# Attention with a mixture of depths on one core: another order of the last products, rows updated product by product, and one scatter a batch

## The chip, the cores and the metric

The kernel runs on one core of a Trainium2 chip. The metric is device microseconds (us) of one execution, less is better. The kernel before was timed three times: 689.43, 689.62 and 692.24 us, with a median of 689.62 us. One more execution was recorded by the hardware profiler. It took 691.44 us in all, of which the trace covers a span of 689.6 us. Moments "at 650.35" are us from the start of that span.

## The reference

```python
# attention with pooled queries: B=8 batches, H=8 heads, S=1152 keys, D=64
q_pool = q.reshape(B, H, S // 2, 2, D).mean(axis=3)          # 576 queries
scores = scale * np.matmul(q_pool, k.transpose(0, 1, 3, 2))
attn = np.exp(scores - max); attn = attn / (sum + 1e-09)
x = np.matmul(attn, v)                                       # -> (B, 576, 512)
# mixture of depths: per batch the 128 best rows go through two dense layers
scores = np.einsum('bsd,d->bs', x, w_gate)
for b in range(B):
    top_idx = np.argpartition(-scores[b], 128)[:128]
    xe = x[b, top_idx]
    h = np.maximum(xe @ w1, 0.0)                             # 512 -> 1024
    ye = h @ w2                                              # 1024 -> 512
    g = 1.0 / (1.0 + np.exp(-scores[b, top_idx]))
    out[b, top_idx] = xe + g[:, None] * ye
```

Everything is float32.

## The kernel before

The order of the work is written out by hand. Each engine runs its instructions in the order in which the program emits them, and waits on semaphores where data come from another engine.

**Main loop** (`run`). Two heads form a pair, and a pair is worked in two halves of 288 queries. Each half has, on TensorE (PE), the scores (L871, 72 records) and the weighted values of the half before (L889, 72 records). ScalarE (ACT) takes the exponential of the scores (L878) and copies the weighted values out (`two`, L897). GpSimd (POOL) adds score tiles (`acc`, L910), adds the two queries of each pool (`qp`, L769), forms the products for the gate (`prod`, L978) and divides (`x`, L1015, `divided`). VectorE (DVE) folds the sums (`fold`, L915) and transposes keys and queries (`kT`, L772, and `qT`, L776). SyncE (SP) issues the loads of keys, queries and values and the stores of `x`, in one queue. PE's next scores need `kT` and `qT`.

**Routing of a batch** (`routed`, a generator). After a batch's last pair its scores are laid out in one line (`line` on DVE; `groups` by four ACT copies, L940; `total` on DVE), written to DRAM and read back to all partitions. DVE ranks them by counting (L1116, L1125, L1135), the 128 best rows are fetched with an indirect DMA on POOL (L1227) and their transpose `xeT` is made. The generator stops at marks: `"mid"`, `"sums"` and `True` (end of the half) say where in the next half the main loop takes it up again (`units`). So work of the routing is spread over later halves, at places fixed by the marks.

**The dense layers** take two batches at once, with Strassen's scheme in Winograd's form: seven products of half-size quarters in place of eight. The text numbers them as the changed kernel does: P1 = a11·b11, P2 = a12·b21, P3 = s1·t1, P4 = s2·t2, P5 = s3·t3, P6 = s4·b22, P7 = a22·t4. The `s` are four sums of quarters of the input, the `t` are sums of weights made early in the kernel, kept in DRAM and loaded into `tw` (`load_sums`, two transfers a layer). Results are sums of products. Batches 0 to 3 go through `layers_of_two` inside the main loop. There, in the kernel before, ACT scales the four result quarters by the gate (L1419), POOL adds them onto the fetched rows `xe` (L1424), and `written` scatters the rows of each batch to `out` with an indirect DMA (L1303).

**The ending** (`ending`) follows the main loop. It holds four layers: the first and second for batches 4 and 5 ("A" and "B" below), and the first and second for batches 6 and 7 ("C" and "D"); A3 is product P3 of layer A. A product of a first layer is 8 matmuls of 128 columns (L1442, two records each), one of a second layer 4 of 256 columns (L1452). PSUM has room for four products at a time (`banks`). Into these products the ending weaves the ranking and fetch of batch 7 (`new`) and the last steps of batch 6 (`old`). Batch 7's ranking needs two small transfers, DVE's counting, one ACT instruction (`gate`, Exp, L1149), ten matmul records that turn ranks into row numbers (L1186), two ACT copies (L1193, L1194), the indirect fetch (`lines<-out_dram,index`, L1227), and four transposes on PE (L1275). In the kernel before, layer B runs P1, P2, P7, P3, P4, P5, P6, with batch 7's row numbers between P4 and P5; POOL makes B's four sums; all B results are combined during C, scaled on ACT and added on POOL. Layer D runs P1, P2, P7, P3 ... P6, batch 6's rows are scattered in two halves of 256 columns, batch 7's in one piece. A scatter waits until the scatter before it has landed, since both write `out`.

In this ending DVE divides the last two pairs' rows (`divided`, L1015); SP stores them.

Of the kernel before, what the change touches and what calls it, by code (L numbers as in the profile page):

```python
# [10 lines left out]
P = 128  # L11
BLK = 32

G = 3
F32 = mybir.dt.float32
I32 = mybir.dt.int32
AF = mybir.ActivationFunctionType
ALU = mybir.AluOpType
# [516 lines left out]
class _Plain:  # L535
# [473 lines left out]
    def divided(self, pair):  # L1009

        x = pair["x"] = self.work.tile([P, self.QB, BLK], F32, name="x")

        ending = pair["b"] == self.B - 1 and pair["hp"] >= self.NPAIR - 2
        engine = self.nc.vector if ending else self.nc.gpsimd
        engine.tensor_tensor(  # L1015
            out=x[:, :, :],
            in0=pair["avb"][:, :, :],
            in1=pair["rec"][:, :].unsqueeze(2).broadcast_to([P, self.QB, BLK]),
            op=ALU.mult,
        )  # L1020
# [39 lines left out]
    def routed(self, b, part):  # L1060
# [11 lines left out]
        )  # L1072
        sc = ffn.tile([P, NT], F32, name="gate_sc")
        if b < self.B - 1:
            yield mid
        groups = self.side_by_side(line)
        if b < self.B - 1:
            yield True
# [297 lines left out]
    def layers_of_two(self, tokens):  # L1376
# [37 lines left out]
        rest = [room[0:w, i, 0:half] for i in (0, 3, 1)]  # L1414
        c = [of[0:w] for of in (c11, c12, c21, c22)]
        yield from self.seven_products(2, quarters(hidden, self.NFC // 2), s, c, rest, lambda bank: bank[0:w, 0:half])
        yield "mid"
        for i, of in enumerate(c):
            nc.scalar.activation(of, of, AF.Copy, scale=tokens[i // 2]["gate"][0:w, 0:1])  # L1419
        yield True  # L1420
        for i, of in enumerate(c):
            token = tokens[i // 2]
            to = token["xe"][0:w, i % 2 * half : (i % 2 + 1) * half]
            nc.gpsimd.tensor_tensor(out=to, in0=of, in1=to, op=ALU.add)  # L1424
            if i % 2:
                self.written(token, token["index"])
                yield True
        if tokens[1]["b"] + 1 < self.paired:
            for _ in self.load_sums(1):
                yield True  # L1430
# [4 lines left out]
    def product(self, layer, of, by, to):  # L1435
# [16 lines left out]
                self.nc.tensor.matmul(to, lhsT=of[:, k, :], rhs=by[:, k, :], start=k == 0, stop=k == n - 1)  # L1452
        return to

    def add(self, to, x, y):
        self.nc.vector.tensor_tensor(out=to, in0=x, in1=y, op=ALU.add)

    def first_layer(self, a, s, c, m):

        copy = self.nc.scalar.copy
        (a11, a12, _, a22), (s1, s2, s3, s4), (c11, c12, c21, c22), (u, w) = a, s, c, m
        b11, b21, b22 = (self.quarter(1, i, j) for i, j in ((0, 0), (1, 0), (1, 1)))
        t1, t2, t3, t4 = (self.summed(1, i) for i in range(4))

        def product(of, by):
            return self.product(1, of, by, self.banks()[:, 0, :])

        def hidden(to, x, y):  # L1470
            self.add(to, x, y)
            self.nc.scalar.activation(to, to, AF.Relu)

        copy(u, product(a11, b11))
        yield
        hidden(c11, u, product(a12, b21))
        yield
        copy(w, product(s1, t1))
        yield
        self.add(u, u, product(s2, t2))  # L1480
        self.add(w, w, u)
        yield
        ps = product(s3, t3)
        hidden(c22, w, ps)
        self.add(u, u, ps)
        yield
        hidden(c12, w, product(s4, b22))
        yield
        hidden(c21, u, product(a22, t4))
        yield  # L1490

    def second_layer(self, a, s):

        (a11, a12, _, a22), (s1, s2, s3, s4) = a, s
        b11, b21, b22 = (self.quarter(2, i, j) for i, j in ((0, 0), (1, 0), (1, 1)))
        t1, t2, t3, t4 = self.last_sums
        for of, by in ((a11, b11), (a12, b21), (a22, t4), (s1, t1), (s2, t2), (s3, t3), (s4, b22)):
            yield self.product(2, of, by, self.banks()[:, 0, :])

    def row(self, tile):  # L1500
        names = "a b c d"[: 2 * len(tile.shape) - 3]
# [4 lines left out]
        n = tiles[0].shape[1] // 2  # L1506
        return [tile[:, i * n : (i + 1) * n, 0:w] for tile in tiles for i in range(2)]

    def four_sums(self, engine, a, room):

        n, w = a[0].shape[1], a[0].shape[2]
        s = [self.lines_of(room[:, i * n * P : (i + 1) * n * P])[:, :, 0:w] for i in range(4)]
        a11, a12, a21, a22 = a
        s1, s2, s3, s4 = s
        add, subtract = ALU.add, ALU.subtract
        for to, x, y, op in ((s1, a21, a22, add), (s2, s1, a11, subtract), (s3, a11, a21, subtract), (s4, a12, s2, subtract)):
            engine.tensor_tensor(out=to, in0=x, in1=y, op=op)
        return s

    def ending(self, halves, old):  # L1520

# [6 lines left out]
                if i + 1 == n:  # L1528
                    break

        def layer_rooms(room):
            return [self.lines_of(room[:, i * half * 2 : (i + 1) * half * 2])[:, :, 0:w] for i in range(2)]

        tokens, a, s = self.left
        w = tokens[0]["w"]
        self.room = self.row(self.work.tile([P, self.NG, G, 2, self.HALF], F32, name="p"))
        acc = [self.row(self.work.tile([P, G, 2 * self.HALF], F32, name="acc"))]
        tiles = [self.ffn.tile([P, self.NFC, P], F32, name="hT") for _ in tokens]
        c = self.quarters_of(tiles, w)
        layer = self.first_layer(a, s, c, layer_rooms(acc[0]))  # L1540

        self.gated(halves[-3])
        pieces(old, 1)
# [14 lines left out]
        for of in (halves[-3]["pair"], last):  # L1558
            self.divided(of)
            self.stored(of)  # L1560
        pieces(layer, 3)
        pieces(new, 1)
        pieces(layer)
        room = self.ffn.tile([P, 4, 512], F32, name="s", bufs=1).rearrange("p a n -> p (a n)")
        s = self.four_sums(nc.gpsimd, c, room)
        acc.append(self.row(self.work.tile([P, G, 2 * self.HALF], F32, name="acc")))
        at = [acc[1][0:w, i * half : (i + 1) * half] for i in range(6)] + [acc[0][0:w, 4 * half : 5 * half]]
        layer = self.second_layer(c, s)
        for to in at[0:2]:
            copy(to, next(layer))  # L1570
        pieces(new, 2)
        for to in at[2:5]:
            copy(to, next(layer))
        pieces(new, 1)
        pieces(old)
        for to in at[5:7]:
            copy(to, next(layer))
        low = self.counted()

        room = self.row(self.work.tile([P, self.NG, G, 2, self.HALF], F32, name="p"))  # L1580
        n = self.NFC * P
        tiles = [self.lines_of(room[:, i * n : (i + 1) * n]) for i in range(2)]
        room = room[:, 2 * n : 4 * n]
        c = self.quarters_of(tiles, w)
        m = self.room[:, 6 * half : 11 * half]
        xeT = [self.lines_of(self.room[:, i * self.Dm : (i + 1) * self.Dm]) for i in range(2)]
        a = self.quarters_of(xeT, w)
        nxt = [self.lines_of(room[:, i * half : (i + 1) * half])[:, :, 0:w] for i in range(4)]
        layer = self.first_layer(a, nxt, c, layer_rooms(m))
        pieces(layer, 1)  # L1590
        pieces(new)
        self.four_sums(nc.vector, a, room)
        m1, m2, m7, m3, m4, m5, m6 = at
        pieces(layer, 1)
        add(m2, m2, m1)
        add(m4, m4, m1)
        pieces(layer, 1)
        add(m3, m3, m4)
        add(m6, m6, m3)
        add(m3, m3, m5)  # L1600
        pieces(layer, 1)
        add(m4, m4, m5)
        add(m7, m7, m4)
        for i, of in enumerate((m2, m6, m7, m3)):
            nc.scalar.activation(of, of, AF.Copy, scale=tokens[i // 2]["gate"][0:w, 0:1])
            to = tokens[i // 2]["xe"][0:w, i % 2 * half : (i % 2 + 1) * half]
            nc.gpsimd.tensor_tensor(out=to, in0=of, in1=to, op=ALU.add)
            if i % 2:
                self.written(tokens[i // 2], tokens[i // 2]["index"])
        pieces(layer, 2)  # L1610
        count = self.outside(low)
        pieces(layer)
        s = self.four_sums(nc.vector, c, room)

        six, seven = tokens = self.last_tokens
        index = [self.part_of_rows(six, part, 2) for part in range(2)]
        to = [token["xe"][0:w, i * half : (i + 1) * half] for token in tokens for i in range(2)]
        u, v, y, z, own = (m[0:w, i * half : (i + 1) * half] for i in range(5))
        found = nc.values_load(count[0:1, 0:1])
        E = mybir.EngineType  # L1620
        self.tc.mark_branch_hint_location("again", found, [E.PE, E.DVE, E.Pool, E.Activation, E.SP])

        def scaled(to, of, token, plus):
            nc.vector.scalar_tensor_tensor(
                out=to, in0=of, scalar=token["gate"][0:w, 0:1], in1=plus, op0=ALU.mult, op1=ALU.add
            )

        layer = self.second_layer(c, s)
        copy(u, next(layer))
        add(own, u, next(layer))  # L1630
        scaled(to[0], own, six, to[0])
        self.written(six, index[0], 0, 2)
        copy(y, next(layer))
        copy(v, next(layer))
        add(u, u, next(layer))
        add(v, v, u)
        scaled(z, v, six, to[1])
        ps = next(layer)
        add(v, v, ps)
        add(u, u, ps)  # L1640
        scaled(to[3], v, seven, to[3])
        add(y, y, u)
        scaled(to[2], y, seven, to[2])
        self.written(seven, seven["index"])
        scaled(to[1], next(layer), six, z)
        self.written(six, index[1], 1, 2)
        return found

    def counted(self):
# [187 lines left out]
```

## Time and profile before

| | us |
|---|---|
| median of three runs (lowest, highest) | 689.62 (689.43, 692.24) |
| the profiled execution | 691.44 |
| its span | 689.6 |
| PE busy | 673.4 |
| DVE busy | 575.0 |
| POOL busy | 516.7 |
| ACT busy | 458.9 |
| main loop, to the first product of the ending | 0 to 624.9 |
| ending | 624.9 to 689.6 |

Lines of the timeline hold the start in us, the duration, the engine, the line of the program, the operation, what is written and read with its shape, and a count. In square brackets stands how long the engine had been idle before it, and what ended that wait. "PEld" is the weight load of PE, which overlaps its matmuls. "PEclk" is the share of its full clock that PE was granted.

### The profile page before, as it was taken

Reading aid. Unit: us, or ns where it says so; the run is one execution under the profiler, and the core shown is the slowest. Engines: PE = TensorE matmul, PEld = TensorE weight load, DVE = VectorE, ACT = ScalarE, POOL = GpSimd, SP = SyncE. Lnnn points to the kernel's source line nnn. Section 1 sums busy time; section 2 is a strip of 40 time slices with the busy share of each in tenths; the row PEclk is TensorE's granted clock in tenths of the full one; section 3 lists DMA queues with packets and bytes.
Section 4 is the critical chain, followed back from the end, with each engine's and each line's share of the span. In section 5 each row is a group of like instructions: output and inputs, shape, how many; then the busy total and the mean of one; then the engine's idle time right before and its main releaser. Section 6 shows DMA issues by size and latency. Waiting matters only on the chain.

```text
span 689.6 us, 23548 instructions
## 1 busy us (share of the span) xinstructions
PE 673.4 (98%) x9953; PEld 455.7 (66%) x9953; DVE 575.0 (83%) x868; ACT 458.9 (67%) x1004; POOL 516.7 (75%) x500
## 2 busy tenths in 40 slices
PE   8999999999999999999999999999999999999994
PEld 6666666666666578676567768667667665668794
DVE  3878998999999986878599996696779998789762
ACT  5677777777777784838777776674877776773130
POOL 4788888879887883848998787393998888973331
PEclk9999999999999999999999999999999999999998
DMA  8888989849995885645898688671898859535100
GB/s 164 168 187 178 221 177 193 156 92 198 202 181 96 182 166 102 175 87 108 204 199 156 132 170 155 136 171 26 176 205 183 166 119 210 136 82 120 38 32 34
DMA packets 396657, 101.49 MB, mean 147 GB/s; under 512 B 376448, under 2 KB 380416, under 8 KB 395520
## 3 DMA queue, kind: packets, MB, share of 16 engines
q1 hardware_dynamic: 395008, 95.43, 67.1%
q0 software_dynamic: 1296, 4.20, 1.8%
q8 instruction: 79, 1.29, 0.8%
q10 hardware_dynamic: 240, 0.30, 0.2%
q14 instruction: 34, 0.28, 0.1%
HBM read 82.27 MB, written 17.62 MB: 145 GB/s over the span
## 4 chain that ended last, share of the span: by engine, by line
PE 76%; DVE 7%; DMA 6%; POOL 5%; issue 3%; ACT 2%; SPq 1%; ACTq 0%; POOLq 0%; DVEq 0%
PE ps L871 33%; PE ps L889 32%; PE ps L1361 7%; PE ps L1442 3%; POOL acc L910 3%; DVE fold L915 2%; ACT p L878 1%; DMA xe<-out_dram,index 1%; DVE kT L772 1%; DMA kb<-in_k_dram 1%; PE ps L1452 1%; POOL out_dram L1303 1%; DMA lines<-row_rank 1%; DVE pick L1125 1%; DVE pick L1135 1%
## 5 line engine op out<-in xcount | busy, mean ns | idle before, releaser
L878 ACT ACTIVATE p<-ps 128x576 f32<-128x576 f32 x576 | 320.7, 691 | 5.3 <-PE ps L871 5.0
L910 POOL TENSOR_TENSOR acc<-p 128x576 f32<-128x576 f32 x192 | 274.8, 1459 | 32.4 <-ACT p L878 32.1
L871 PE MATMUL ps<-qT,kT 64*64 64x288 f32 x4608 | 293.6, 404 | 4.1 <-DVE qT L776 2.1
L889 PE MATMUL ps<-p,v_sb 64*64 64x288 f32 x4608 | 291.6, 403 | 0.0
L871 PEld LDWEIGHTS ps<-qT,kT 64*64 64x64 f32 x4608 | 177.1, 132 | 108.3 <-ACT p L878 20.5
L889 PEld LDWEIGHTS ps<-p,v_sb 64*64 64x64 f32 x4608 | 176.9, 133 | 102.9 <-ACT p L878 14.3
L915 DVE TRANSPOSE_TENSOR_REDUCE fold<-p 128x54 f32<-128x1728 f32 x64 | 126.0, 1968 | 28.9 <-ACT p L878 28.4
L915 DVE TRANSPOSE_TENSOR_REDUCE fold<-acc 128x54 f32<-128x1728 f32 x64 | 124.6, 1946 | 22.7 <-POOL acc L910 22.5
L897 ACT COPY two<-ps 128x576 f32<-128x576 f32 x64 | 40.9, 638 | 132.7 <-PE ps L889 116.4
L899 POOL TENSOR_TENSOR av<-two 128x288 f32<-128x288 f32 x64 | 51.8, 810 | 69.3 <-ACT two L897 69.2
L772 DVE STREAM_TRANSPOSE kT<-kb 128x1152 f32<-128x1152 f32 x31 | 72.9, 2353 | 0.0
L978 POOL TENSOR_TENSOR prod<-avb,w_gate 128x288 f32<-128x288 f32 x64 | 51.9, 811 | 1.7 <-DVE red L1037 1.5
L769 POOL TENSOR_TENSOR qp<-qb 128x576 f32<-128x576 f32 x31 | 43.8, 1412 | 3.0 <-DMA qb<-in_q_dram 3.0
L968 DVE STREAM_TRANSPOSE avb<-av 128x288 f32<-128x288 f32 x64 | 28.6, 447 | 18.2 <-POOL av L899 18.2
L955 ACT ACTIVATE sums<-total,tiny 32x18 f32<-32x18 f32 x124 | 38.2, 308 | 4.6 <-DVE total L946 2.8
L1015 POOL TENSOR_TENSOR x<-avb,rec 128x576 f32<-128x576 f32 x30 | 34.8, 1159 | 0.0
L1135 DVE SCALAR_TENSOR_TENSOR pick<-sc_row,gate_sc,before 128x128 f32<-128x128 f32 (+1 forms) x40 | 31.8, 795 | 1.4
L940 ACT COPY groups<-sum 32x36 f32<-32x36 f32 x124 | 27.0, 218 | 2.7 <-DVE sum L925 1.2
L1037 DVE TENSOR_REDUCE red<-prod 128x9 f32<-128x288 f32 x64 | 27.8, 434 | 0.1
L925 DVE TENSOR_REDUCE sum<-fold 128x18 f32<-128x108 f32 x64 | 21.9, 342 | 2.2
L776 DVE STREAM_TRANSPOSE qT<-qp 128x576 f32<-128x576 f32 x31 | 23.0, 741 | 0.0
L1125 DVE TENSOR_SCALAR_CACHE_REDUCE pick<-sc_row,gate_sc 128x576 f32<-128x576 f32 (+4 forms) x40 | 21.6, 539 | 0.3
(176 smaller groups left out, 480.0 us busy)
## 6 DMA issues: line engine op xcount, KB each, us to landing
kb<-in_k_dram SPq DMA_DIRECT2D x124, 144.0 KB, 4.4
qb<-in_q_dram SPq DMA_DIRECT2D x124, 144.0 KB, 3.8
v_sb<-in_v_dram SPq DMA_DIRECT2D x31, 576.0 KB, 6.5
out_dram<-x SPq DMA_DIRECT2D x128, 72.0 KB, 4.7
tw<-tw SPq DMA_DIRECT2D x8, 1024.0 KB, 5.4
lines<-row_rank SPq DMA_DIRECT2D x7, 640.0 KB, 4.8
w<-in_moe_w_dram SPq DMA_DIRECT2D x8, 512.0 KB, 6.7
tw<-tw SPq DMA_DIRECT2D x8, 512.0 KB, 4.8
```

Of the source, the lines that this page charges most:

```text
L769: nc.gpsimd.tensor_tensor(out=qp[:, :, :], in0=pair["q"][:, :, 0, :], in1=pair["q"][:, :, 1, :], op=ALU.add)
L772: nc.vector.transpose(kT.rearrange("p (c i g) -> p c g i", c=self.NC, i=BLK), pair["k"].rearrange("p (g c) d -> p c g d", c=self.NC),)
L871: nc.tensor.matmul(sc[keys, j, 0:n], lhsT=pair["kT"][rows, c * P + keys.start : c * P + keys.stop], rhs=pair["qT"][rows, qs], start=True, ...
L878: nc.scalar.activation(p[:, c // G, c % G, :, :], sc[:, :, 0:n], AF.Exp, scale=self.scale)
L889: nc.tensor.matmul(av[j * self.D : (j + 1) * self.D, e, 0:n], lhsT=half["pair"]["v"][keys, j, c, :], rhs=half["p"][keys, c // G, c % G, j, :],
L897: nc.scalar.copy(two[:, :, :], av[:, :, 0:n])
L899: nc.gpsimd.tensor_tensor(out=half["av"][:, :], in0=two[:, 0, :], in1=two[:, 1, :], op=ALU.add)
L910: nc.gpsimd.tensor_tensor(out=acc[:, u, :], in0=units[:, 0, u, :], in1=units[:, 1, u, :], op=ALU.add)
L915: nc.vector.tensor_reduce(fold[:, a, :], of.rearrange("p u (m d) -> p (u m) d", d=BLK), AX.X, ALU.add, apply_transpose=True,)
L978: self.nc.gpsimd.tensor_tensor(out=pair["prod"][:, ns, :], in0=pair["avb"][:, ns, :], in1=self.w_gate[:, hp : hp + 1, :].broadcast_to([P, ...
L1135: nc.vector.scalar_tensor_tensor(out=tie[0:rows, 0:rows], in0=sc_row[0:rows, at : at + rows], scalar=own, in1=self.before[0:rows, 0:rows], ...
L1361: nc.tensor.matmul(args[0], lhsT=args[1], rhs=args[2], start=k == 0, stop=k == n - 1)
```

## The change

Seven edits, all of order and of place:

1. In `routed`, for batch 6 alone, the four ACT copies of `groups` are taken up at `"mid"` of the next half and not at the end of the present one.
2. In `layers_of_two` (batches 0 to 3) the ACT scalings and POOL additions are gone. DVE does both in one instruction for each quarter (`scaled`, 128x256), two in the "mid" of each of two halves. One stop is left out, and the stops are placed so that both transfers of `load_sums(1)` are issued one after the other, ahead of the next keys; before, the second came one half later.
3. In the ending, POOL does the last two divisions, and DVE makes B's four sums.
4. Batch 6's transpose of `xeT` comes before A5. A7's result is kept by an ACT copy, and its addition comes after batch 7's ranking.
5. After B1, B2 and B7 the products C1 and C2 run ahead of batch 7's row numbers. B3, B4 and B5 follow, then the transposes of batch 7's rows, then B6. B's results update the rows of batches 4 and 5 on DVE as they come.
6. D runs P1, P7, P3, P4, P5, P6, P2, and DVE adds each product to the rows as it comes, scaled by the gate.
7. Batch 6 is scattered in one piece, after batch 7.

```diff
@@ divided
-        ending = pair["b"] == self.B - 1 and pair["hp"] >= self.NPAIR - 2
-        engine = self.nc.vector if ending else self.nc.gpsimd
-        engine.tensor_tensor(
+        self.nc.gpsimd.tensor_tensor(
@@ routed
         if b < self.B - 1:
-            yield mid
+            yield "mid"
         groups = self.side_by_side(line)
@@ layers_of_two
-        yield "mid"
-        for i, of in enumerate(c):
-            nc.scalar.activation(of, of, AF.Copy, scale=tokens[i // 2]["gate"][0:w, 0:1])
-        yield True
         for i, of in enumerate(c):
             token = tokens[i // 2]
+            if i % 2 == 0:
+                yield "mid"
             to = token["xe"][0:w, i % 2 * half : (i % 2 + 1) * half]
-            nc.gpsimd.tensor_tensor(out=to, in0=of, in1=to, op=ALU.add)
+            self.scaled(to, of, token, to)
             if i % 2:
-                self.written(token, token["index"])
                 yield True
+                self.written(token, token["index"])
@@
+    def scaled(self, to, of, token, plus):
+        self.nc.vector.scalar_tensor_tensor(
+            out=to, in0=of, scalar=token["gate"][0 : token["w"], 0:1], in1=plus, op0=ALU.mult, op1=ALU.add
+        )
@@ ending
-        pieces(layer, 3)
-        pieces(new, 1)
-        pieces(layer)
-        s = self.four_sums(nc.gpsimd, c, room)
-        for to in at[0:2]:
-            copy(to, next(layer))
-        pieces(new, 2)
-        for to in at[2:5]:
-            copy(to, next(layer))
-        pieces(new, 1)
-        pieces(old)
-        for to in at[5:7]:
-            copy(to, next(layer))
-        low = self.counted()
...
+        pieces(layer, 1)
+        pieces(old)
+        pieces(layer, 3)
+        second = self.second_layer(c, s, (1, 2, 7, 3, 4, 5, 6))
+        for to in (y1, y2, y7):
+            copy(to, next(second))
...
+        pieces(third, 1)
+        pieces(new, 3)
+        pieces(layer)
+        self.four_sums(c, s)
+        pieces(third, 1)
+        pieces(new, 1)
+        copy(y3, next(second))
+        self.add(y2, y2, y1)
+        self.scaled(to[0], y2, four, to[0])
+        self.add(y4, y1, next(second))
+        self.add(y3, y3, y4)
+        self.add(y4, y4, y7)
+        ps = next(second)
+        pieces(new)
+        self.four_sums(a, sums)
...
-        self.written(six, index[0], 0, 2)
...
+        second = self.second_layer(of_tiles, s, (1, 7, 3, 4, 5, 6, 2))
...
+        self.scaled(to[3], ps, seven, to[3])
+        self.scaled(to[2], ps, seven, to[2])
         self.written(seven, seven["index"])
-        scaled(to[1], next(layer), six, z)
-        self.written(six, index[1], 1, 2)
+        self.scaled(to[1], next(second), six, to[1])
+        self.scaled(to[0], next(second), six, to[0])
+        self.written(six, six["index"])
```

## The prediction

> **What bounds the kernel now.** First the page's busy times and its chain, to see which engine sets the end.
>
> ```profile
> PE 673.4 (98%) x9953; PEld 455.7 (66%) x9953; DVE 575.0 (83%) x868; ACT 458.9 (67%) x1004; POOL 516.7 (75%) x500
> ...
> PE 76%; DVE 7%; DMA 6%; POOL 5%; issue 3%; ACT 2%; SPq 1%; ACTq 0%; POOLq 0%; DVEq 0%
> ```
>
> PE is busy for 673.4 of 689.6 us and holds 76% of the chain. The matmuls stay, so only PE's gaps, its clock and the tail behind its last product can change. Then the timeline around PE's gaps in the main loop. Batch 6's line copies:
>
> ```profile
> 576.91 0.85 ACT L940 COPY groups<-line 32x18 f32<-32x18 f32 x4 [0.98 <-DVE line L1070]
> ...
> 577.67 4.89 ACT L878 ACTIVATE p<-ps 128x576 f32<-128x576 f32 x9
> ...
> 578.36 2.84 PE L871 MATMUL ps<-qT,kT 64*64 64x288 f32 x40 [1.26 <-ACT p L878]
> ```
>
> ACT waits 0.98 for `line` and copies for 0.85 before it empties PSUM; PE stands for 1.26. Next the update of batches 0 and 1, the first of two such rounds:
>
> ```profile
> 313.49 4.16 POOL L910 TENSOR_TENSOR acc<-p 128x576 f32<-128x576 f32 x3 [1.14 <-ACT p L878]
> 313.49 1.49 DVE L1135 SCALAR_TENSOR_TENSOR pick<-sc_row,gate_sc,before 64x64 f32<-64x64 f32 x1
> ...
> 335.76 1.06 POOL L1303 DMA_INDIRECT out_dram<-xe,index  x1 [1.20 <-DMA xe<-out_dram,index]
> ...
> 346.82 3.58 PE L871 MATMUL ps<-qT,kT 64*64 64x288 f32 x53 [1.08 <-DVE qT L776]
> ```
>
> POOL's second scatter waits for a fetch; `acc`, fold, `kT` and `qT` follow, and PE stands 1.08 (1.00 in the round of batches 2 and 3). Last the ending, its clock by stretches (columns: length, then busy us of PE, PEld, DVE, ACT, POOL; the last three are the granted clock, the DMA share and GB/s) and its timeline:
>
> ```profile
> 647.10:650.60 3.50, 2.06 (x14) 1.98 (x15) 3.01 (x4) 0.58 (x3) 0.26 (x1) 1.00 0.00 0
> 650.60:654.00 3.40, 3.40 (x10) 2.64 (x9) 0.84 (x4) 0.37 (x1) 0.78 (x1) 0.50 0.29 82
> ```
>
> ```profile
> 649.92 0.16 ACT L1193 CAST index<-ps 128x1 int32<-128x1 f32 x1 [2.46 <-PE ps L1186]
> ...
> 650.35 1.04 POOL L1227 DMA_INDIRECT lines<-out_dram,index  x1 [3.57 <-ACT own_gate L1194]
> ...
> 659.10 5.52 PE L1442 MATMUL ps<-p,tw 128*128 128x128 f32 x48
> ...
> 678.83 1.89 PE L1452 MATMUL ps<-w,p 128*128 128x256 f32 x8
> ...
> 681.31 0.98 POOL L1303 DMA_INDIRECT out_dram<-lines,index  x1 [6.53 <-DVE lines L1624]
> 684.83 0.98 POOL L1303 DMA_INDIRECT out_dram<-xe,index_part  x1 [2.53 <-DMA out_dram<-lines,index]
> ```
>
> PE stands 1.44 around batch 7's ranks, then has half its clock for 3.4 us. From C3 (659.10) to the end of D6 (678.83 + 1.89 = 680.72) it never rests. The last scatter follows 4.11 later, since it waits for the one before.
>
> **Batch 6's copies: -1.26.** They move behind the next half's `sums`, where ACT stood idle 1.87 before `two` at 585.74; DVE's `total` needs them only at 588.28. PE's 1.26 goes; the halves after it are PE's, and DVE follows ACT's earlier exponentials (it waited 1.94 and 2.50 for them). Ends 0 and -1.8 (all of 0.98 + 0.85).
>
> **Rows of batches 0 to 3 on DVE: -1.0.** Each round sheds four POOL additions of 0.69 (321.84 and 332.56) and four ACT scalings in idle time. POOL's first scatter comes 2 x 0.69 + 0.29 = 1.66 earlier, and so `acc`, the fetch and the second scatter, which keeps its place about 0.8 behind the fetch's landing. That alone closes the gap: -1.08 and -1.00. [...] The row is L1135: 0.28 us at its shortest, 1.49 here under `acc`. [...] Ends per round -1.08 and +1.5; I take -0.5, half of the gain.
>
> **The second `tw` transfer ahead of keys: 0.** SP's copy out of `xe` waits for the fetch; behind it now stand two transfers of 1 MB (5.4 to land) and then keys, `pick`, queries, values and stores, all some 5 later. Cover: keys issued at 336.0 feed `kT` at 358.0, queries issued 344.6 to 349.1 feed `qp` at 355.86, values issued at 349.18 feed L889 at 359.94. The values landed 4.9 after their issue by the trace's landing records, so 0 to 1 of slack is left there. One half later the queue is 1 MB lighter. Ends 0 and +2.
>
> **The ending, on the clock of the trace.** A to A7 stays PE's (638.4). B1, B2, B7 at 1.73 and C1, C2 at 1.79 follow without a gap, to 647.1; `xeT` of batch 6 is ready at 635.5, DVE having lost the two divisions (1.41). Ranking: POOL's divisions may hold the small `part` (630.15) by 0.7 to 1.9, but that is not what ends last. Gate Exp, at 642.18 before, now stands on ACT behind the copies of B1, B2, B7 and C1: 645.3 + 0.59 gives 645.9 to 646.1. DVE gets there about 644 (its tie at 641.71 and gate at 645.58, 1.26 and 1.22 under POOL's sums, fall to 0.35 and 0.17) and waits. Then 0.17 + 0.19 + 0.13 + `pick` 1.29: 647.8, against 648.40. The rank matmuls end at 649.3.
>
> Behind them the change adds a wait. The index copies stand on ACT behind the ReLU of A7 and that of C2, and C2's addition stands on DVE behind B's four sums: 647.8 + addition 0.68 + ReLU 0.63 + sums 4 x 0.66 + addition 0.69 + ReLU 0.63 is 653.0 with the gaps between engines. Index at 653.0, not 649.92. The fetch is issued about 653.3, lands 3.72 later (as 650.35 to 654.07) at 657.1. PE runs B3, B4, B5 from 649.9 to 655.1 and stands until 657.2, then transposes (0.64) and B6 (1.73): C3 at 659.6, 0.5 later than now.
>
> From there the same 21.4 us of products: D2 ends at 680.9. D's order matters at the tail. Batch 7 is complete with D5, 3.45 before; DVE is five instructions behind there, so the scatter goes at 679.2, lands 2.74 later (681.9), and batch 6's follows 0.77 behind (684.06 to 684.83 now): 682.7. Its rows are whole, so 2.74 and not 2.43 to land. Now 684.83 + 2.43; then 682.7 + 2.74: -1.8 for the ending. Layer D's first two products cover its sums (667.2 to 669.9 on DVE); with P1, P7 alone that is 3.45 for 3.3 needed until the first, so 0.
>
> **The clock.** Without the half clock the ending before is faster: its two products from 649.81 to 655.05 take 5.24, not 3.46, and 1.6 of it reaches C3 (657.5). Changed, the same stretch falls on B3 to B5, ahead of a wait of 2.1, and costs nothing. [...] The trace shows less idleness to be enough (1.44 of 3.5, plus rank matmuls of two columns), and gaps of 1.08 and 1.26 not to be. [...] I take 0.
>
> **The sum.** Against the profiled 691.44: -1.26 - 1.0 - 1.8 = 687.4. The median lies 1.8 below the profiled time, about what its half clock costs, so I read the median as without it: there the ending is worth -0.2, and 689.62 - 1.26 - 1.0 - 0.2 = 687.2. I forecast 687.2.
>
> **Rivals.** (a) All gaps close and the runs before had the half clock too: -1.26 - 2.1 - 1.8 gives 684.5. For it: the profile has it. Against: two of three runs are 1.8 or more below it. (b) The new gap before the transposes halves the clock: 688.9. For: 2.1 is longer than the gap that did it. [...] (c) Slower: DVE's updates wait out POOL's `acc`, `index` comes late, and fetch, scatter, `acc`, `qT` are later than before, with no slack in front of PE; at +2.0 a round 689.62 - 1.46 + 4.0 = 692.2. It decides from +0.7 a round. For: L1135's 1.49. Against: POOL is lighter by 2.8 a round. (d) The second `tw` transfer reaches PE through values or queries, +1 a round: 689.2.
>
> **How the numbers follow.** Chances: forecast 0.42, (a) 0.26, (b) 0.14, (c) 0.11, (d) 0.07. Below 686.17, faster by over 0.5% (about what a measurement of this kernel can tell from no change), lie most of (a) and a fifth of the forecast: 0.32. Above 693.07 lies a part of (c): 0.07. The rest, 0.61. Range 684.0 to 690.6: it takes in (a), (b), (d) and (c) up to +1.2 a round.
>
> **What would show it.** Right: no gap at the L871 of batch 6's line; L871 after the second scatter within 0.6 of gapless; index at 3 behind its old place against A7's end; PE standing about 2 before L1275; last scatter under 2 us behind PE's last product. Wrong: `scaled` in the loop above 1 us and a gap over 1.8 there; half clock over C3; values landing after their L889 could start.

## The result, and the profile after

The changed kernel took 689.00 us in the median (685.72 to 691.56, 14 runs), beside 689.66 (687.81 to 692.24, 14 runs) of the kernel before on the same chip. The ratio is 0.9979, with a 95% interval of 0.9961 to 0.9997: no change by the bound of 0.5%. The forecast was 687.2 in a range of 684.0 to 690.6, with 0.61 on no change.

The profiled execution took 688.71, with a span of 686.9, against 691.44 and 689.6: 2.7 less. These are two single executions: the one of the kernel before was 1.8 slower than its median, so the medians lie only 0.7 apart. The page of the changed kernel, its busy times and its chain:

```profile
PE 674.0 (98%) x9953; PEld 461.5 (67%) x9953; DVE 591.3 (86%) x880; ACT 454.7 (66%) x989; POOL 501.1 (73%) x485
...
PE 81%; DVE 6%; DMA 5%; issue 3%; POOL 2%; ACT 1%; SPq 1%; ACTq 0%; POOLq 0%; DVEq 0%
```

POOL is lighter by 15.6 us and DVE heavier by 16.3. 12.6 of that is DVE held up inside its own instructions: the two first searches (2.86 and 2.87, free 0.83), one second search (5.13, free 0.80) and four of the row updates (6.14 together, free 1.92). PE is as busy as before, so what the change moved lies in a few places. I read them from the start of each run of L871 on PE in both traces, after minus before (negative is earlier):

| place | step |
|---|---|
| L871 at 232 (5.02 before, 4.66 after; nothing of the change is near) | -0.36 |
| round of batches 0 and 1, to 345.39 | -1.08 |
| in between, at 408 | +0.09 |
| round of batches 2 and 3, the gap at 513 | +1.51 |
| the L871 behind that gap | +1.69 |
| two small steps, at 548 and 575 | -0.46 |
| batch 6's copies, 576 to 585 | -1.72 |
| from the merge product at L991 to the end of the span (62.4 before, 60.0 after) | -2.4 |
| sum | -2.7 |

So most of what was gained was lost again in one place, the round of batches 2 and 3. The timeline of the changed kernel at L871 behind the second scatter of both rounds, at batch 6's line, and in the second round on DVE and POOL:

```profile
345.39 4.60 PE L871 MATMUL ps<-qT,kT 64*64 64x288 f32 x72 [0.40 <-DVE qT L776]
...
499.59 1.05 POOL L1300 DMA_INDIRECT out_dram<-xe,index  x1 [2.01 <-DVE fold L915]
500.38 5.13 DVE L1197 SCALAR_TENSOR_TENSOR pick<-lines,token 128x640 f32<-128x640 f32 x1
500.67 4.14 POOL L910 TENSOR_TENSOR acc<-p 128x576 f32<-128x576 f32 x3
...
513.39 6.29 PE L871 MATMUL ps<-qT,kT 64*64 64x288 f32 x72 [2.51 <-DVE qT L776]
...
576.41 4.54 PE L871 MATMUL ps<-qT,kT 64*64 64x288 f32 x72
...
583.57 0.85 ACT L940 COPY groups<-line 32x18 f32<-32x18 f32 x4
```

The 576.41 line has no bracket: batch 6's gap is gone, and the copies stand at 583.57 behind the next half's `sums`. The first round's gap fell from 1.08 to 0.40. The second round's grew from 1.00 to 2.51. The line to look at is 500.38. It is the second `search` of `routed`, by which DVE picks the gate of each fetched row. The timeline of the kernel before at the same place:

```profile
499.85 2.00 POOL L1424 TENSOR_TENSOR xe<-s,xe 128x256 f32<-128x256 f32 x2
500.46 0.80 DVE L1200 SCALAR_TENSOR_TENSOR pick<-lines,token 128x640 f32<-128x640 f32 x1
...
503.21 4.15 POOL L910 TENSOR_TENSOR acc<-p 128x576 f32<-128x576 f32 x3
```

There the search took 0.80, and POOL's three `acc` came at 503.21, 2.75 after it had begun. Now they begin at 500.67, 0.29 after it, and it takes 5.13, to 0.70 behind the last of them. The folds, `kT` and `qT` are queued behind it. And the L871 takes 6.29, not 4.60. The clock by stretches of the changed kernel (the column after the five engines' busy times is the granted clock) shows the half clock there and in the ending:

```profile
511.07:514.50 3.43, 1.11 (x20) 0.90 (x24) 3.43 (x5) 2.31 (x9) 3.43 (x4) 1.00 0.81 155
514.50:517.93 3.43, 3.43 (x36) 2.36 (x32) 3.40 (x3) 2.68 (x5) 1.93 (x4) 0.50 0.98 157
648.27:651.70 3.43, 2.87 (x15) 2.52 (x15) 2.79 (x5) 0.57 (x1) 0.00 (x0) 0.90 0.02 5
651.70:655.13 3.43, 3.43 (x11) 2.73 (x11) 1.27 (x4) 1.01 (x4) 1.03 (x1) 0.60 0.08 16
```

After the stretch in which PE stood 2.3 of 3.4 us, the next has half the clock. The ending, on the timeline of the changed kernel:

```profile
645.57 0.21 ACT L1146 ACTIVATE gate<-gate 128x5 f32<-128x5 f32 x1
646.29 1.29 DVE L1174 TENSOR_TENSOR pick<-token_line,rank 128x640 f32<-128x640 f32 x1
...
652.73 0.14 ACT L1190 CAST index<-ps 128x1 int32<-128x1 f32 x1
653.13 1.03 POOL L1224 DMA_INDIRECT lines<-out_dram,index  x1 [21.58 <-ACT own_gate L1191]
656.75 0.72 PE L1272 MATMUL ps<-ident,lines 128*128 128x128 f32 x4
659.03 3.17 PE L1437 MATMUL ps<-p,tw 128*128 128x128 f32 x27
...
678.64 0.98 POOL L1300 DMA_INDIRECT out_dram<-lines,index  x1 [12.40 <-DVE lines L1451]
682.14 0.98 POOL L1300 DMA_INDIRECT out_dram<-xe,index  x1 [2.52 <-DMA out_dram<-lines,index]
```

The index is 2.81 later than the 649.92 of before, C3 starts at 659.03 (659.10 before), and the last scatter goes out at 682.14, not at 684.83.

### The profile page after: what moved, and what is told of

The parts are those of the page before. It is cut to its first block, busy times and chain, and to the rows that moved or that the text cites. A ratio compares the mean times of both kernels' runs of the same rounds, so it can differ in the third digit from the quotient of the medians.

```text
span 686.9 us, 23530 instructions
## 1 busy us (share of the span) xinstructions
PE 674.0 (98%) x9953; PEld 461.5 (67%) x9953; DVE 591.3 (86%) x880; ACT 454.7 (66%) x989; POOL 501.1 (73%) x485
## 3 DMA queue, kind: packets, MB, share of 16 engines
q8 instruction: 79, 1.29, 0.8%
## 4 chain that ended last, share of the span: by engine, by line
PE 81%; DVE 6%; DMA 5%; issue 3%; POOL 2%; ACT 1%; SPq 1%; ACTq 0%; POOLq 0%; DVEq 0%
PE ps L871 36%; PE ps L889 34%; PE ps L1358 7%; PE ps L1437 2%; PE ps L1447 2%; DMA kb<-in_k_dram 1%; POOL acc L910 1%; DVE fold L915 1%; DVE kT L772 1%; DMA lines<-row_rank 1%; DMA p<-in_q_dram 1%; DMA xe<-out_dram,index 1%; ACT p L878 1%; DMA gate_sc<-row 1%; DMA row<-total 0%
## 5 line engine op out<-in xcount | busy, mean ns | idle before, releaser
L871 PE MATMUL ps<-qT,kT 64*64 64x288 f32 x4608 | 294.1, 405 | 3.6 <-DVE qT L776 2.9
L889 PE MATMUL ps<-p,v_sb 64*64 64x288 f32 x4608 | 291.5, 403 | 0.0
L871 PEld LDWEIGHTS ps<-qT,kT 64*64 64x64 f32 x4608 | 181.0, 133 | 104.4 <-ACT p L878 14.7
L889 PEld LDWEIGHTS ps<-p,v_sb 64*64 64x64 f32 x4608 | 178.6, 133 | 100.9 <-ACT p L878 13.5
L1012 POOL TENSOR_TENSOR x<-avb,rec 128x576 f32<-128x576 f32 x32 | 37.0, 1156 | 0.0
```

What stands on the lines that cost most here:

```text
L871: nc.tensor.matmul(sc[keys, j, 0:n], lhsT=pair["kT"][rows, c * P + keys.start : c * P + keys.stop], rhs=pair["qT"][rows, qs], start=True, ...
L889: nc.tensor.matmul(av[j * self.D : (j + 1) * self.D, e, 0:n], lhsT=half["pair"]["v"][keys, j, c, :], rhs=half["p"][keys, c // G, c % G, j, :],
```

## The experiments

Ratios are against the kernel before on the same chip; its median was 689.66, 689.29, 690.70 and 691.62 in the four groups of runs. Gaps are PE's in front of the L871 of the two rounds and of batch 6's line; a star marks half a clock behind it. "Ending" is the time from the merge product (L991 in the kernel before) to the end of the span.

| kernel | median | lowest to highest | ratio (95%) | gaps | ending |
|---|---|---|---|---|---|
| before (profile) | | | | 1.08 / 1.00 / 1.26 | 62.4 |
| changed | 689.00 | 685.72 to 691.56 | 0.9979 (0.9961 to 0.9997) | 0.40 / 2.51* / 0 | 60.0 |
| e1 copies back | 690.43 | 687.13 to 692.42 | 1.0011 (0.9991 to 1.0030) | 0.48 / 2.28 / 1.31 | 60.0 |
| e2 search early | 684.37 | 683.89 to 684.87 | 0.9934 (0.9921 to 0.9947) | 0.16 / 0.37 / 0 | 60.0 |
| e3 rows back | 685.34 | 684.52 to 685.99 | 0.9945 (0.9933 to 0.9958) | 0.84 / 0 / 0 | 60.0 |
| e4 index early | 685.35 | 684.07 to 686.29 | 0.9942 (0.9927 to 0.9957) | 1.11 / 2.46 / 0 | 56.9 |
| e6 copies alone | 687.59 | 686.01 to 690.12 | 0.9970 (0.9954 to 0.9986) | 0.80 / 0.68 / 0 | 62.5 |
| e8 ending alone | 687.93 | 686.73 to 690.00 | 0.9969 (0.9950 to 0.9988) | 1.51 / 1.60 / 2.02* | 59.8 |
| e10 rows alone | 692.26 | 687.59 to 695.16 | 1.0016 (0.9986 to 1.0046) | 0.39 / 0.34 / 2.03* | 62.3 |
| e5 tables later | 686.79 | 684.52 to 693.15 | 0.9960 (0.9935 to 0.9986) | 1.23 / 0.51 / 0 | 61.1 |
| e12 changed again | 686.70 | 685.02 to 689.92 | 0.9948 (0.9926 to 0.9971) | 2.86* / 1.25 / 0 | 59.9 |
| e7 search and index early | 681.66 | 680.41 to 683.75 | 0.9865 (0.9836 to 0.9894) | 0.82 / 0.97 / 0 | 56.7 |
| e11 index early, rows back | 682.73 | 681.09 to 684.05 | 0.9878 (0.9849 to 0.9906) | 0.42 / 0.77 / 0 | 56.9 |

### e1 and e6: batch 6's copies

```diff
 (e1, from the changed kernel; e6 is the reverse, from the kernel before)
-            yield "mid"
+            yield mid
         groups = self.side_by_side(line)
```

> The changed kernel with one part undone: batch 6's four line copies on ACT stand ahead of ACT's emptying of the next bank again, as before. Theory: this part is worth what stood in the trace of before there; the gap returns in front of the L871 of batch 6's line (1.0 to 1.3, put down to ACT) and that half's L871 products take 6.0 from their first start to the first L889 behind them, not 4.36. The time rises by 1.3 to 1.7 against the changed kernel: about 690.4. Rival (the part is hidden work): PE's later halves wait anyway, the time stays at 689.0.

> The kernel before with only the move of batch 6's line copies. Theory: the same 1.3 to 1.7 that the changed kernel lost without it (690.43 against 689.0): PE has no gap at that L871, the time is 687.7 to 688.3 against some 689.5 of the kernel before. Rival: before's own halves there wait for something else, the time stays within 0.5.

The mechanism is as the theory had it, the gain a little larger. Without the move the gap is back at 1.31 and the median is 1.4 above the changed kernel's; with it alone the kernel before gains 2.1 (0.9970 of 690.70), where 1.3 to 1.7 was expected. In every trace with the move, the way from that L871 to the next is 1.72 shorter than in the trace of before. The gap is only 1.26 of it: the L871 split by the gap also ran slower (2.84 for the 40 records behind the gap in the kernel before, 71 ns each, against 4.54 for 72, 63 ns each, in the changed kernel). (e1's profile has a gap of 2.28 in the second round without half a clock behind it.)

### e2: the own-gate search out of POOL's way

```diff
-                if b == self.B - 2:
-                    search(lines[:, :, 1, :], own_gate)
+                search(lines[:, :, 1, :], own_gate)
...
-            if b < self.B - 2:
-                search(lines[:, :, 1, :], own_gate)
```

> The changed kernel, in which DVE's second search (the own gate of batches 0 to 5, 0.80 us free) runs directly behind the computation of the index and no longer behind the folds of the next half. Seen in the changed kernel's profile: in the round of batches 2 and 3 this search starts at 500.38, POOL's three sums at 500.67, and the search takes 5.13; the folds, keys and queries behind it are late, PE stands 2.51 and then has half its clock for 3.4 us. Theory 1 (the search is caught by POOL's sums, which start earlier since POOL lost its additions): the search takes 0.8 to 1.0, the gap of that round falls to 0.5 or less, no half clock there; -2.3 to -4 in a profile that has both, and a median of 685.5 to 687. Theory 2 (the second table transfer stands ahead of the keys): nothing changes, gap 2 to 2.5, median 689. Theory 3 (the row updates themselves, 1.44 and 1.63 under POOL's sums, not 0.48): the gap stays at about 2, median 688.5 to 689.

Theory 1, and by more than it claimed. The timeline of e2 in the second round:

```profile
493.38 0.88 DVE L1197 SCALAR_TENSOR_TENSOR pick<-lines,token 128x640 f32<-128x640 f32 x1
493.74 1.46 POOL L1223 DMA_INDIRECT xe<-out_dram,index  x1 [1.16 <-DVE index L1209]
...
500.05 4.16 POOL L910 TENSOR_TENSOR acc<-p 128x576 f32<-128x576 f32 x3
...
510.06 4.60 PE L871 MATMUL ps<-qT,kT 64*64 64x288 f32 x72 [0.37 <-DVE qT L776]
```

The search takes 0.88 while POOL waits for the index, PE waits 0.37, and the L871 takes 4.60, not 6.29. Table loads and row updates stand where the changed kernel has them, so theories 2 and 3 fall as the cause of that gap. The five runs lie within 1.0, against 5.8 in the changed kernel's fourteen; the kernel before, in which no search is caught, spreads by 4.9 beside them, so the spread by itself proves nothing.

### e3 and e10: the rows of batches 0 to 3

e3 puts the loop of the kernel before back into the changed kernel (it is the "-" part of `layers_of_two` in the diff above); e10 puts the new loop alone into the kernel before.

> The changed kernel with the rows of batches 0 to 3 updated as before: scaled on ACT, added on POOL, the tables loaded one half later. Theory (rows on DVE: a gain in the first round, a loss in the second): the gaps return to 1.08 and 1.00, against 0.40 and 2.51 plus 1.7 of half clock; the first round loses 0.7, the second gains 1.5 to 3.2, so the time is 686.5 to 688.3. Rival (the sum of the prediction: DVE's rows are worth 0.5 a round): the time rises by 1.0, to 690.0.

> The kernel before with only the rows of batches 0 to 3 updated on DVE (one instruction for scaling and addition, the table loads one half earlier). Theory (the own-gate search is caught by POOL's sums in the round of batches 2 and 3): the search takes about 5 there, PE stands 2 to 2.5 in front of that round's L871, sometimes with half a clock behind it; the time rises by 1 to 3.5, to 690.5 to 693. Rival (the sum of the prediction): -1.0, 688.5. If only the changed ending and copies shift the phases so that the search is caught, the time stays within 0.5 of before.

With the rows back on ACT and POOL the changed kernel took 685.34, better than the 686.5 to 688.3 expected, and opposite to the prediction's sum. Part of that is not the rows': e3's second round has no gap where the kernel before has 1.00, and there its first scatter held POOL for 1.11 and not 2.06, so that the fetch went at 495.25 and not at 497.24. Why that issue takes now the one and now the other was not tried.

e10 missed in its profile: the search was not caught there. The timeline of e10, second round:

```profile
494.38 1.06 POOL L1227 DMA_INDIRECT xe<-out_dram,index  x1 [1.16 <-DVE index L1212]
499.54 1.06 POOL L1303 DMA_INDIRECT out_dram<-xe,index  x1 [2.50 <-DVE sum L925]
499.83 0.78 DVE L1200 SCALAR_TENSOR_TENSOR pick<-lines,token 128x640 f32<-128x640 f32 x1
500.63 4.15 POOL L910 TENSOR_TENSOR acc<-p 128x576 f32<-128x576 f32 x3
...
510.64 4.60 PE L871 MATMUL ps<-qT,kT 64*64 64x288 f32 x72 [0.34 <-DVE qT L776]
```

The search ends at 500.61, POOL's sums begin at 500.63. Both rounds gain here, 0.93 and 0.66 against the trace of before. The times of the runs stand apart: four of twelve lie at 687.6 to 688.2, seven at 692.0 to 695.2, and the profiled one at 689.9. I read this as a race (two chains of work start together, and now the one, now the other is first), which e12 was to show. The spread alone does not show it: the seven longest have a mean granted clock of 0.988 to 0.993 and the four shortest 0.996, but the kernel before, without the race, lies at 687.5 to 694.8 in the same group, with clocks of 0.987 to 0.997.

### e12: the changed kernel again

> The changed kernel once more, unaltered, beside the two that follow, since its runs lie between 685.7 and 691.6. Theory (DVE's own-gate search and POOL's sums race in the round of batches 2 and 3: a fetch that takes 4.5 to 4.7 from its issue to the second scatter lets the sums catch the search, one that takes 5.2 or more does not): in the profile either 4.5 to 4.7, a search of about 5 and a gap of 2.3 to 2.5, or 5.2 and more, a search of 0.8 and a gap of 0.3 to 0.6; the median 687 to 689.5, a range of 5 or more.

In this profile the second round went well (5.71 from fetch to scatter, search 0.79), though its gap was 1.25 and not 0.3 to 0.6, and the first did not. The timeline of e12, first round:

```profile
328.65 1.06 POOL L1224 DMA_INDIRECT xe<-out_dram,index  x1 [1.16 <-DVE index L1209]
333.67 1.05 POOL L1300 DMA_INDIRECT out_dram<-xe,index  x1 [2.37 <-DVE sum L925]
...
334.09 5.50 DVE L1197 SCALAR_TENSOR_TENSOR pick<-lines,token 128x640 f32<-128x640 f32 x1
334.76 4.14 POOL L910 TENSOR_TENSOR acc<-p 128x576 f32<-128x576 f32 x3
...
347.45 4.81 PE L871 MATMUL ps<-qT,kT 64*64 64x288 f32 x48 [2.86 <-DVE qT L776]
```

The same accident, one round earlier, and again half a clock behind it (48 records in 4.81, 100 ns each; a mean of 0.65 in 346.43 to 349.86). In all kernels with the rows on DVE and the search in its old place, the search starts 5.44 to 5.45 after the fetch is issued: `index` sets DVE and POOL off together. The second scatter, and `acc` 1.08 behind it, come when the fetch has landed. Where the scatter came 4.48 (e1), 4.65 (e4), 4.66 (changed) or 5.02 (here) after the fetch's issue, the sums caught the search; at 5.16 (e10), 5.27 and 5.34 (the changed kernel's first round, e5) it got through. So my bound of 4.7 was too low: in these rounds the search was caught when `acc` started within its 0.8. There a fetch that lands sooner makes the kernel slower. In the rounds in which the search got through (with e2's and e7's), a later fetch costs: the gap is 0.16 to 0.51 where the second scatter came 5.03 to 5.34 after the fetch's issue, and 0.82 to 1.25 where it came 5.71 to 6.02 after. So relieving POOL did not close the gap even there, since the second scatter waits for the fetch.

The median of 686.70 is a little under what was expected, the range of 4.9 just under the 5 expected. The two measurements of the changed kernel, 0.9979 and 0.9948, have intervals that overlap between 0.9961 and 0.9971.

### e5: the table loads

```diff
+            yield True
             for _ in self.load_sums(1):
                 yield True
```

> The changed kernel with both table loads behind the second scatter put one half later, so that one transfer of 1 MB and not two stands ahead of the keys, as before. Theory (the round's gap comes from the search under POOL's sums): the gaps stay at 0.4 and 2.3 to 2.5, the search at about 5, the time within 0.7 of 689.0. Rival (the second transfer delays keys and queries): the gap of the round of batches 2 and 3 falls below 1.2, the time to 686.5 to 687.5.

Inconclusive. The numbers are those of the rival: the second round's gap fell to 0.51 and the median is 686.79. But the second scatter came 5.34 after the fetch's issue there and the search got through, so the gap says nothing of the loads; and the ratio's interval overlaps both of the changed kernel's. What the traces say of the loads stands below.

### e8: the ending alone

This is the kernel before with all edits in `divided`, `ending` and the functions that it calls.

> The kernel before with only the change of the ending (order of products, updates product by product, one scatter a batch). In the traces the time from the first product of the ending to the end of the span is 62.4 before and 59.95 to 60.0 in the changed kernel and in three of its variants, whether or not the clock halves behind the ranks. Theory: the ending is worth 2.4, since most runs of the kernel before had the half clock too: 687.1. Rival (the prediction's reading of the median as without the half clock): -0.2, 689.3.

0.9969 is 2.1 of 690.70: the theory, not the rival. Its profile shows something else as well. The timeline of e8:

```profile
578.39 4.06 PE L871 MATMUL ps<-qT,kT 64*64 64x288 f32 x40 [2.02 <-ACT p L878]
```

Batch 6's gap, 1.26 in the trace of before, can be 2.02 with half a clock behind it (0.50 in 579.67 to 583.10). e10's 2.03 is the same. So the move of the copies also takes away a place where the clock halves in some runs.

### e4: the index earlier in the ending

```diff
+        pieces(new, 3)
         for to in (y1, y2, y7):
             copy(to, next(second))
...
-        pieces(new, 3)
         pieces(layer)
-        self.four_sums(c, s)
         pieces(third, 1)
         pieces(new, 1)
+        self.four_sums(c, s)
```

> The changed kernel with two moves in its ending: batch 7's gate exponential is put on ACT ahead of the copies of the products B1, B2, B7 and C1, and DVE's four sums of layer B's input come behind C2's addition, so that the index copies on ACT no longer wait for them. The order on PE stays. Theory (the index is late because of what stands ahead of it in ACT's and DVE's queues): pick ends at 646.2 and not 647.6, index at about 648.5 and not 652.7, the fetch lands about 652.6, PE stands neither before the rank matmuls (0.89) nor before the transposes (1.4 to 1.9), C3 starts at 656 to 657 and not 659.0; the time falls by 2 to 3, to 686 to 687. Rival (the sums are late instead: B3 waits for them): C3 moves by less than 1, the time stays within 1 of 689.0.

The timeline of e4:

```profile
644.72 1.33 DVE L1174 TENSOR_TENSOR pick<-token_line,rank 128x640 f32<-128x640 f32 x1
...
648.08 0.14 ACT L1190 CAST index<-ps 128x1 int32<-128x1 f32 x1
648.49 1.26 POOL L1224 DMA_INDIRECT lines<-out_dram,index  x1 [17.05 <-ACT own_gate L1191]
...
653.45 0.63 PE L1272 MATMUL ps<-ident,lines 128*128 128x128 f32 x4
655.65 5.52 PE L1437 MATMUL ps<-p,tw 128*128 128x128 f32 x48
...
678.76 0.98 POOL L1300 DMA_INDIRECT out_dram<-xe,index  x1 [2.51 <-DMA out_dram<-lines,index]
```

The steps came as the theory had them, and a little earlier: pick ends at 646.05, the index is at 648.08, PE waits neither for ranks nor for rows, C3 starts at 655.65 (656 to 657 expected), and the ending is 56.9 long. The median, 685.35, lies below the 686 to 687 expected. No half clock is left there: B3 to B5 take 1.99, 1.89 and 1.89.

### e7 and e11: the two together

e7 is e4 with e2's earlier search; e11 is e4 with e3's rows.

> The changed kernel with the own-gate search directly behind the index, the gate exponential of batch 7 ahead of the copies on ACT and the four sums of layer B behind C2's addition. Theory: the two gains add, 4.6 in the rounds and 3.1 in the ending (56.9 and not 60.0 from the first product of the ending to the end of the span): 681.3, in a range of 1 to 1.5. Rival: the ending's gain in its own run came partly from a clock that did not halve elsewhere: 682.5 to 683.5.

> The same earlier index in the ending, but the rows of batches 0 to 3 scaled on ACT and added on POOL as before, in place of the earlier search. Theory: no search is caught, the second scatter waits for POOL's additions, the gaps are 0.5 to 1.0: 682.3, about 1 above the one with the earlier search, in a range of 1 to 2. Rival (the rows on DVE were the whole harm and nothing of it is left with the earlier search): the same time as that one within 0.3.

The gains add, as far as this measurement can tell: 681.66 where 681.3 was expected, 1.35% below the kernel before (0.9836 to 0.9894), the fastest of all. e11 is 1.07 behind it, as e3 was 0.97 behind e2. That suggests that, with the race out of the way, the updates on DVE together with the earlier search beat ACT and POOL by about 1.0; the intervals overlap in both pairs, and e11's traced execution (683.79) lost 1.45 to half a clock at 7.75, which no edit touches, so it is not shown. The earlier search on its own, with POOL's additions, was not tried.

## Why the prediction was right, and where it was wrong

"No change" and the range held, but in part by luck: errors of opposite sign lie inside the number, a loss in the rounds where a gain was forecast, and gains at batch 6 and in the ending that were put too low. One sign of being wrong that the prediction names came true as well: `scaled` in the loop above 1 us (1.44 and 1.63) with a gap above 1.8 (2.51).

**Batch 6's copies, -1.26: mechanism right, size low.** 1.72 in every trace with the move. The sum took the gap and left out that the L871 split by it was slower (71 ns a record behind it, not 63). That the gap could halve the clock was not weighed, since 1.26 had not done so; in e8 and e10 the gap is 2.0 and the clock halves.

**Rows on DVE, -1.0: wrong.** The row set against the gain, L1135's 1.49, was the right one, and the updates themselves fared like it: 1.44 and 1.63 under `acc`, 0.48 free; POOL's `part` waited 0.73 for `red`, and the first scatter came 0.97 sooner and not 1.66 (322.58 for 323.55, 0.34 of it gained earlier). The step that failed is the sentence that the second scatter comes earlier with `acc` behind it and that "that alone closes the gap". The two rounds were to give -1.0 together; in the trace of the changed kernel they cost +2.1 (-1.08, +1.51 and +1.69 for the half clock). The other end, +1.5 a round, was my estimate, and no run shows it as a cost of the updates; the +1.51 of the second round came behind the search. I listed what waits for POOL, and not what POOL's earlier sums would land on. DVE's searches run beside POOL's instructions too, and the trace of before had a sign of what that costs: beside the search at 500.46, POOL's two additions took 2.00, and at 488.73, with no search beside them, 0.74 and 0.73. The first search took 2.86 and 2.87, not 0.83, so the first round's fetch came only 0.93 sooner (329.03 for 329.96), 0.34 of it gained earlier. The second was caught in one round of four of the six profiles that could show it. When it gets through, a round gains 0.1 to 0.9 (e12's second round loses 0.25). When it is caught, the round loses 1.3 to 1.5, or 3.2 with the half clock. Rival (c) forecast a loss in the rounds (+2.0 each, where one gained 1.1 and one lost 3.2), but from a late `index`, and named neither search.

**The second `tw` transfer, 0: not refuted.** Values were issued at 349.82 (349.18 before) and landed at 355.07 (354.12), some 3.4 ahead of their L889. SP waited in its keys' issues, so what lies behind them came 0.6 later, not the 5 that I feared. e5 doesn't settle it, but e2 bounds it: with both transfers ahead of the keys, PE waits 0.16 and 0.37 in its two rounds, and nowhere over 0.3 between and behind them in the main loop.

**The ending, steps right.** Shifted by the 0.34 by which the ending starts sooner, the forecast was pick 647.5, index 652.7, C3 659.3, D2's end 680.6, last scatter 682.4. Measured: 647.58, 652.73, 659.03, 680.53, 682.14. The last transfer needed no more than before (4.7 from its issue to the end of the span, 4.8 before); I had given it 0.3 more. So -2.4, where the sum said -1.8.

**The choice between the two routes: wrong.** I read the median of before as a run without the half clock and took -0.2 for the ending. e8 measured -2.1, and the three profiles with the old ending (before, e6, e10) all have the half clock behind batch 7's ranks (means of 0.66, 0.63 and 0.58 in the slowest stretch of 3.43), at 62.3 to 62.5. What the 1.8 between the profiled time and the median was stays open, since only one execution of the kernel before was traced. With -1.8 for the ending the sum would have been 685.6; e2 (684.37) and e3 (685.34), without the loss in the rounds, lie near that.

**The clock.** That the half clock would fall on B3 to B5 at no cost held: 60.0 with it, and in e1, without it, 60.0 too, with PE standing 1.62 ahead of the transposes. Not always: in e5 it lasts over B3 and B4 (3.78 and 3.16 for 1.89 each) and the ending is 1.1 longer. The 0 taken for the gap ahead of the transposes, and the 1.7 by which rival (b) lies above the forecast, were my estimates. No trace has the half clock over C3, so no run shows that 1.7, and rival (b) did not occur there. In the main loop the clock did halve: the gaps of 2.02, 2.03, 2.51 and 2.86 were followed by half a clock, those of 2.28 and 2.46 (e1, e4) were not. The traces show what parted them. In each trace the half-clock stretches ahead of the tail last 3.41 (twice that in e5) and start whole multiples of 3.413 apart (514.49 and 651.02 in the changed kernel: 40 of them), so the time can be laid out in such windows. Here are the windows with the long gaps of e4 and e8, each with the one behind it:

```profile
512.68:516.09 3.41, 1.56 (x28) 1.23 (x32) 3.41 (x5) 2.32 (x8) 3.41 (x4) 1.00 0.75 156
516.09:519.50 3.41, 3.41 (x64) 2.45 (x60) 3.38 (x4) 3.41 (x7) 2.60 (x5) 1.00 1.02 168
...
576.26:579.67 3.41, 1.39 (x24) 0.62 (x24) 3.38 (x6) 2.69 (x8) 1.42 (x2) 1.00 0.98 143
579.68:583.09 3.41, 3.41 (x32) 1.80 (x28) 0.98 (x3) 3.09 (x6) 3.08 (x3) 0.50 0.99 198
```

From 340 to 620 us the clock halved behind the windows in which PE stood 2.03 (e8 and e10), 2.31 (changed) and 2.86 (e12), and behind none with 1.85 (e4) or less. e4's gap of 2.46 fell on two windows, with 0.61 and 1.85; e1's 2.28 fell as 0.99 and 1.29. So in these traces a gap a little above 2 halved the clock when it lay in one window, and where the windows lie differs from trace to trace. At the start of the kernel and around batch 7's ranks, with smaller matmuls, less idleness was enough in some traces (1.49 in e11 at 4.33, 0.68 in the changed kernel at 647.61) and not in others (1.50 in e7 at 4.24, 0.89 in e1 at 645.33); what parts these stays open. My estimate from these traces is that a term of 1.7 (half of the 3.41) times a chance of a half or more belonged to every gap above 2 in the main loop of this kernel (four of six).

## What to carry to other kernels

When an engine is relieved, list not only who waits for its results but also what its next instructions will run beside, and look in the trace for instructions of the other engine that are long only in such company. Where two chains start from one event and the order of their ends decides which is held up, take more than one trace, since one may show only one of the two orders, and move one of them out of the way; here that was worth more than the edit itself. The spread of the runs is no sign by itself: the kernel before, without the race, spread by 4.4 to 7.3. In an ending, walk each queue for what stands ahead of the instruction on the critical path: two reorderings on ACT and DVE shortened it by 3.1.

## What the runs showed of the hardware

- DVE's 128x640 search (0.80 free) took 2.83 to 2.90 in the two rounds with two of POOL's sums left to run, and 4.94 to 5.50 with three. It ended 0.70 behind the last, and the sums took 4.14, as with no search beside them (4.15 at 503.21 in the kernel before). In e12 it had begun 0.67 before the first sum and still needed that 0.70 behind the last, so the earlier start did not spare it the wait. The 128x256 updates ended between two sums (1.44, with POOL's three at 4.33). So in these rounds the search was held up to the end of two or three sums in a row. But the size doesn't decide it: in other rounds the same search ended between two sums (1.88 at 166.89 in e6, where POOL's three sums then took 4.73), and in e8 it was held up longer in the same place (3.00 at 167.97). What decides it stays open.
- Half a clock of 3.41 us behind gaps of 2.0 to 2.9 in four of six cases (changed, e8, e10, e12; not e1, e4), those in which one window of 3.41 had PE idle for 2.03 or more. In e12's runs those with a mean clock of 0.999 took 685.0 to 686.9 and those with 0.993 took 689.1 to 689.9.
